# One zero region of a decode backward kernel, written by a memory-to-memory copy on 4 rows and two smaller stores

## The chip, the cores and the metric

The kernel runs on one core of one Trainium2 chip. The metric is device time in microseconds (us) of one execution; lower is better. Times of the kernel before are given as the median of three executions.

## The reference, cut to what matters

One decode step of a block with attention over a sliding window and a gated feed-forward network, and its gradients. Only the last W = 1024 of Sk = 4096 rows of the caches take part:

```python
W = min(4096, max(256, Sk // 4))
k = jnp.repeat(k_cache[:, :, Sk - W:, :], rep, axis=1)
v = jnp.repeat(v_cache[:, :, Sk - W:, :], rep, axis=1)
...
_out, _vjp = jax.vjp(_f, A_x, A_k_cache, A_v_cache, A_wq, A_wo, B_w_gate, B_w_up, B_w_down)
_grads = _vjp(grad_out)
return (_out0, *[jnp.asarray(_g) for _g in _grads])
```

B = 4 sequences, 8 kv-heads, 32 query heads, head size 128, all bf16. Outputs are y, dx, dK cache (`out_2`), dV cache (`out_3`), dWq, dWo and the three feed-forward weight gradients. The gradients of the caches have the full shape (4, 8, 4096, 128). Their first K0 = Sk - W = 3072 rows of each sequence and kv-head are zero, because those rows don't take part. These zeros are 2 x 32 x 3072 x 128 x 2 bytes = 50.3 MB (32 stores of 1536 KB) of the 81.01 MB that the kernel writes.

## The kernel before

**Tiling.** The attention part runs in NT = 4 steps `t` of GP = 2 kv-heads each. A step loads K and V of its two heads (one DMA of 1 MB each per head for all four sequences), transposes the blocks on TensorE (L352), makes scores and the gradient of the probabilities (L345), runs the softmax chain on small tiles, and gives back dK and dV blocks (`dvdk`, L475) and the weight gradients (`dw`, L498). The feed-forward network comes ahead of it, with the same scheme.

**Stores.** Every store goes through `store` (L100). It issues a DMA from SyncE (SP) with `dma_start` and declares that stores of the groups "rest" and "zeros" write disjoint parts of the outputs. dK and dV are gathered in a staging tile `stg`, of which there are three (L719); a tile is stored with one DMA of 1 MB when all JQ blocks are in it (L487 to L489), and its next user waits for that DMA.

**Zeros.** `ztile` (L158) is one SBUF tile of zeros, 128 partitions of 12 KB. `zlist` (L159) lists 32 regions (tensor, sequence, pair of kv-heads). `zero(n)` (L161) takes the next n regions off its left end and writes each with one DMA of 1536 KB, 128 rows of 12 KB, all from `ztile`. The calls of `zero` are spread over the program by hand: ahead of the loads, after each dK and dV store (L490), in the background pieces of the feed-forward network, a group of four in the last step (L734), and what is left at the end (L755).

**Order.** Work that may run in the gaps of other work is put as small functions in the queue `bg`; `tick(n)` (L262) takes n of them. `chain` and `link` do the same for the softmax steps. In the last step, t = 3, the order around the change is: the second K/V pass `kv_steps(t, 1, 1)` (L732) with the pieces of dK and weights of step 2 in its gaps, then `zero(4)` (L734), then the rest of the chain, `softmax_d`, `odq` and `fin` with the dV pieces of step 3 in the gaps. The first dV store of step 3 follows the four zero stores on SP. After the loop, `tick(len(bg))` (L754) gives the last dK and weight pieces.

**Queue.** SP issues its DMAs in program order and waits ahead of each for what it needs. Eight completion semaphores are used in turn for the DMAs issued from SP and ScalarE, and a DMA waits until the earlier DMA on its semaphore has landed. The last two results, `out_b` (L769) and `dx_b` (L787), 4 rows of 1 KB each, are issued from ScalarE.

Of the kernel before, what the change touches and what calls it, by code (L numbers as in the profile page):

```python
# [14 lines left out]
P = 128  # L15
# [3 lines left out]
def kernel(  # L19
# [28 lines left out]
    nc = tc.nc  # L48

    B, Sq, D = A_x.shape  # L50
    _, G, Sk, Dh = A_k_cache.shape
# [4 lines left out]
    K0 = Sk - W  # L56
# [43 lines left out]
    def store(eng, out, in_, kind):  # L100

        eng.nop()
        d = eng.dma_start(out=out, in_=in_)
        for k in ("rest", "zeros") if kind == "rest" else ("rest",):
            tc.declare_no_dep(d.ins, group=k, reason="stores write disjoint parts of the outputs")
        tc.add_to_no_dep_group(kind, d.ins)
        return d
# [12 lines left out]
    def load_w(t, eng=nc.gpsimd):  # L120
        pool = w_pool[t % 2]
        wo_t[t] = pool.tile([P, HG, D], BF16, name="wo_sb", tag="wo")
        eng.dma_start(out=wo_t[t][:], in_=wo_v[t])
        wq_t[t] = pool.tile([P, ND, CW], BF16, name="wq_sb", tag="wq")
        eng.dma_start(out=wq_t[t][:], in_=wq_v[t])

    def load_kv(t, k):
        if t >= NT:
            return
        d_, src, nm = ((k_t, A_k_cache, "kb"), (v_t, A_v_cache, "vb"))[k]  # L130
        for g in range(GP):
            tl = kv_pool[t % 2].tile([P, JB, Dh], BF16, name=nm, tag=nm)
            nc.sync.dma_start(out=tl[:].rearrange("p j d -> p (j d)"),
                              in_=src[:, t * GP + g, K0:Sk, :].rearrange("b (m j) d -> m b (j d)", j=JB))
            d_[(t, g)] = tl
# [22 lines left out]
    ztile = const.tile([P, ZW], BF16, name="ztile")  # L158
    zlist = deque((og, b, g) for b in range(B) for g in range(0, G, ZR) for og in (out_2, out_3))  # L159

    def zero(n=1):  # L161
        for _ in range(min(n, len(zlist))):
            og, b, g = zlist.popleft()
            store(nc.sync, og[b, g:g + ZR, 0:K0, :].rearrange("g (m j) d -> m g (j d)", m=P // ZR), ztile[:], "zeros")


    nc.gpsimd.memset(ztile[:], 0.0)
    zero(3)
    ident_f = const.tile([P, P], FP32, name="ident_f")
    nc.vector.tensor_copy(out=ident_f[:], in_=ident[:])  # L170
# [91 lines left out]
    def tick(n):  # L262
        for _ in range(min(n, len(bg))):
            bg.popleft()()
# [3 lines left out]
    def link(n=1):  # L268
        for _ in range(min(n, len(chain))):
            chain.popleft()()  # L270
# [64 lines left out]
    def kv_steps(t, k, links):  # L335

        zt = (qm_all, dom_all)[k][t % 2]
        blks = (k_t, v_t)[k]
        ps = ps_a.tile([P, WQ], FP32, name="S_ps", tag=("S", "dP")[k])
        st[t][("S", "dP")[k]] = ps[:]  # L340

        def mm(g, q, T_sb):
            c0 = SL - 1 - (g * NQ + q)
            for b in range(B):
                nc.tensor.matmul(ps[b * RB:(b + 1) * RB, :], lhsT=zt[:, b * GP + g, c0:c0 + RB],  # L345
                                 rhs=T_sb[:].rearrange("p (x b) -> p b x", b=B)[:, b, :], start=(g == 0 and q == 0),
                                 stop=(g == GP - 1 and q == NQ - 1), tile_position=(0, b * RB))

        last = None
        for g in range(GP):  # L350
            for q in range(NQ):
                T_ps = transposes([blks[(t, g)][:, q * JQ + j, :] for j in range(JQ)], "T")  # L352
                T_sb = tsb.tile([P, JQ * P], BF16, name="T_sb", tag="T")
                evac(T_sb[:], T_ps[:].rearrange("p j x -> p (j x)"), 1024, half=True)
                tick(1)
                link(links)
                if last:
                    mm(*last)
                last = (g, q, T_sb)
                tick(1)  # L360
                link(links)
        mm(*last)
# [104 lines left out]
    def odT(t, k):  # L467
        rows = st[t][("o", "dq")[k]]
        T_ps = transposes([rows[:, g, :] for g in range(GP)], "odT")
        rT = attw.tile([P, GP, B, rep], BF16, name="od_T", tag=f"od_T{k}")  # L470
        for g in range(GP):
            nc.vector.tensor_copy(out=rT[:, g].rearrange("p b r -> p (b r)"), in_=T_ps[:, g, g * 32:g * 32 + B * rep])
        st[t][("oT", "dqT")[k]] = rT
# [243 lines left out]
    with tc.tile_pool(name="kv_b", bufs=GP, reuse_waits="tile") as kv_b, \  # L717
            tc.tile_pool(name="w_b", bufs=1, reuse_waits="tile") as w_b, \
            tc.tile_pool(name="stage", bufs=3, reuse_waits="tile") as stage:  # L719
        kv_pool[1], w_pool[1] = kv_b, w_b  # L720
        zero()
        pre(0)
        load_w(1)
        load_kv(1, 0)
        for t in range(NT):
            kv_steps(t, 0, 0)
            if t == 0:
                zero()
                load_kv(1, 1)
                zero()  # L730
            softmax(t)
            kv_steps(t, 1, 1)  # L732
            if t == NT - 1:
                zero(4)  # L734
            link(len(chain))
            softmax_d(t)
            link()
            odq(t, 0)
            load_kv(t + 2, 1)
            if t + 1 < NT:  # L740
                pre(t + 1)
            link(len(chain))
            odT(t, 0)
            odq(t, 1)
            load_kv(t + 2, 0)
            tick(2)
            odT(t, 1)
            fin(t)
            if t + 2 < NT:
                load_w(t + 2)  # L750
            (k0, k1), (o0, o1, q0, q1) = dvdk(t, 1), dw(t)
            for p in (k0, o0, k1, o1, q0, q1):
                bg.extend(p)
        tick(len(bg))  # L754
        zero(len(zlist))  # L755

        fin_ps = []
        for o in range(2):
            f_ps = ps_w.tile([B, ND, P], FP32, name="f_ps", tag="w")
            for c in range(ND):  # L760
                nc.tensor.transpose(f_ps[:, c, :], acc[:, o, c, :], ident_f[:])
            fin_ps.append(f_ps)
        acc_o = fin_ps[0][:].rearrange("b c p -> b (c p)")
        acc_d = attw.tile([B, P, ND], FP32, name="acc_d", tag="P_s")
        nc.vector.tensor_copy(out=acc_d[:].rearrange("b p c -> b c p"), in_=fin_ps[1][:])
        acc_d = acc_d[:].rearrange("b p c -> b (p c)")
        out_b = attw.tile([B, D], BF16, name="out_b", tag="pT")
        nc.vector.tensor_tensor(out=out_b[:], in0=acc_o, in1=x4[:], op=ALU.add)
        nc.scalar.dma_start(out=out_0.rearrange("b s d -> (b s) d"), in_=out_b[:])  # L769

        s1 = attw.tile([B, 1], FP32, name="s1", tag="m")
        nc.vector.reduce_sum(out=s1[:], in_=acc_d, axis=AX.X)
        pr = attw.tile([B, D], FP32, name="pr", tag="dS_s")
        s2 = attw.tile([B, 1], FP32, name="s2", tag="es")
        nc.vector.tensor_tensor_reduce(out=pr[:], in0=acc_d, in1=xn_f[:], scale=1.0, scalar=0.0,
                                       op0=ALU.mult, op1=ALU.add, accum_out=s2[:])
        nm1 = attw.tile([B, 1], FP32, name="nm1", tag="rr")
        nc.vector.tensor_scalar(out=nm1[:], in0=s1[:], scalar1=-1.0 / D, scalar2=None, op0=ALU.mult)
        nm2 = attw.tile([B, 1], FP32, name="nm2", tag="gs")
        nc.vector.tensor_scalar(out=nm2[:], in0=s2[:], scalar1=-1.0 / D, scalar2=None, op0=ALU.mult)  # L780
        nc.vector.scalar_tensor_tensor(out=pr[:], in0=xn_f[:], scalar=nm2[:, 0:1], in1=acc_d,
                                       op0=ALU.mult, op1=ALU.add)
        nc.vector.tensor_scalar(out=pr[:], in0=pr[:], scalar1=nm1[:, 0:1], scalar2=rstd[:, 0:1],
                                op0=ALU.add, op1=ALU.mult)
        dx_b = attw.tile([B, D], BF16, name="dx_b", tag="E_f")
        nc.vector.tensor_tensor(out=dx_b[:], in0=pr[:], in1=dy4[:], op=ALU.add)
        nc.scalar.dma_start(out=out_1.rearrange("b s d -> (b s) d"), in_=dx_b[:])  # L787
# [30 lines left out]
```

## Time and profile before

| what | value |
|---|---|
| times of three executions | 282.87, 282.91, 283.6 us; median 282.91 us |
| profiled execution, its own time | 283.0 us |
| span of its instructions | 281.0 us |
| busy: TensorE / VectorE / ScalarE / GpSimd | 203.1 / 164.1 / 117.8 / 40.1 us |
| moved by the DMA engines | 112.12 MB, mean 399 GB/s |
| HBM read / written by the program | 30.68 / 81.01 MB |
| zero stores | 32 of 1536 KB, median 18.1 us from issue to landing |
| granted TensorE clock | 0.901 of full speed |

The span runs from the first to the last instruction that the profile shows; the time of the execution is 2.0 us longer. A DMA's "landing" is the time at which the last of its 16 completion counts arrived. The core has 16 DMA engines. Each DMA is cut into packets, one row of the transfer or part of it per packet, and the trace records start, duration, size and queue of each packet, but not the engine that moved it.

### The profile page before, as it was taken

To read this page: it belongs to the slowest core of one execution; us is meant where nothing else is said; L and a number is where in the kernel's file an instruction comes from. 1 tells how busy PE (TensorE), PEld (TensorE's weight loads), DVE (VectorE), ACT (ScalarE), POOL (GpSimd) and SP (SyncE) were. 2 spreads that over 40 slices of the span, in tenths; PEclk is the share of its full clock that TensorE was granted. 3 is DMA by queue.
4 is the path that set the end of the run, shared out by engine and by line. 5 is a ranking of instruction groups with operands and counts; after the bars stand their busy time and mean duration, and the time that the engine had idled before them with its cause. 6 is when DMAs were issued, how large, how long until landed. Compare 5 with 4: busy or idle time off the path is not lost.

```text
span 281.0 us, 6867 instructions
## 1 busy us (share of the span) xinstructions
PE 203.1 (72%) x2972; PEld 138.8 (49%) x2972; DVE 164.1 (58%) x313; ACT 117.8 (42%) x219; POOL 40.1 (14%) x40
## 2 busy tenths in 40 slices
PE   0276699959789889998999299898999599390000
PEld 0265476735456665566775156677556484140000
DVE  7946646645776655577666067767677728386000
ACT  2030386635035418764448056443866038370000
POOL 8600000007002150002250000223000400000000
PEclk9999589986999999999999969999999979977555
DMA  7999999999999999999999999999999999999990
GB/s 264 393 375 431 431 426 417 425 419 424 369 395 424 422 420 420 426 415 422 419 417 411 412 424 423 431 383 398 385 368 415 387 432 410 425 429 422 398 422 30
DMA packets 19565, 112.12 MB, mean 399 GB/s; under 512 B 1664, under 2 KB 4496, under 8 KB 11088
## 3 DMA queue, kind: packets, MB, share of 16 engines
q1 hardware_dynamic: 17744, 103.56, 89.6%
q0 software_dynamic: 1632, 6.29, 5.6%
q10 hardware_dynamic: 160, 1.84, 1.9%
q8 instruction: 23, 0.38, 0.5%
q14 instruction: 6, 0.05, 0.0%
HBM read 30.68 MB, written 81.01 MB: 397 GB/s over the span
## 4 chain that ended last, share of the span: by engine, by line
PE 47%; DMA 22%; DVE 16%; ACT 4%; issue 2%; SPq 0%; DVEq 0%; ACTq 0%
DMA out_dram<-stg_dv 13%; PE T_ps L279 8%; PE kv_ps L484 7%; DMA wd_sb<-in_B_w_down_dram 6%; PE S_ps L345 5%; PE od_ps L450 5%; DMA out_dram<-osb_g 4%; DVE T_sb L98 3%; DVE dS_s L367 2%; PE wdT_ps L279 2%; PE dwq_ps L520 2%; PE acc_ps L256 2%; PE dwd_ps L660 2%; DVE P_s L367 2%; PE wgT_ps L279 2%
## 5 line engine op out<-in xcount | busy, mean ns | idle before, releaser
L98 DVE COPY T_sb<-T_ps 128x1024 bf16<-128x1024 bf16 x64 | 44.1, 688 | 26.7 <-PE T_ps L279 26.5
L97 ACT CAST stg_dk<-kv_ps 128x512 bf16<-128x512 f32 x52 | 29.2, 588 | 31.2 <-PE kv_ps L484 12.4
L97 ACT CAST stg_dv<-kv_ps 128x512 bf16<-128x512 f32 x51 | 28.1, 588 | 24.9 <-PE kv_ps L484 24.3
L484 PE MATMUL kv_ps<-qmr,dS_s 128*128 128x512 bf16 x64 | 23.9, 414 | 11.3 <-ACT stg_dk L97 10.6
L463 POOL TENSOR_TENSOR o_s<-od_r,msk_r 128x512 bf16<-128x512 bf16 x8 | 9.1, 1157 | 110.2 <-DVE od_r L455 80.9
L484 PE MATMUL kv_ps<-domr,P_s 128*128 128x512 bf16 x64 | 21.3, 382 | 0.0
L279 PE MATMUL T_ps<-ident,vb 128*128 128x128 bf16 x256 | 20.3, 225 | 0.4 <-DVE T_sb L98 0.4
L279 PE MATMUL T_ps<-ident,kb 128*128 128x128 bf16 x256 | 20.4, 225 | 0.0
L279 PEld LDWEIGHTS <-kb 128*128 128x128 bf16 x256 | 17.5, 101 | 4.5 <-issue 1.3
L279 PEld LDWEIGHTS <-vb 128*128 128x128 bf16 x256 | 17.2, 101 | 5.0 <-issue 3.2
L97 ACT CAST osb_q<-dwq_ps 128x512 bf16<-128x512 f32 x25 | 14.6, 587 | 8.3 <-PE dwq_ps L520 7.4
L329 POOL TENSOR_TENSOR domr<-r,msk 128x1024 bf16<-128x1024 bf16 x4 | 7.6, 1892 | 71.2 <-DVE r L326 65.1
L97 ACT CAST osb_g<-dwg_ps 128x512 bf16<-128x512 f32 (+1 forms) x25 | 12.3, 544 | 12.3 <-PE dwg_ps L673 6.3
L97 ACT CAST osb_o<-dwo_ps 128x512 bf16<-128x512 f32 x24 | 13.9, 586 | 4.5 <-PE dwo_ps L505 2.9
L98 DVE CAST stg_dk<-kv_ps 128x512 bf16<-128x512 f32 x12 | 8.0, 688 | 12.0 <-DMA out_dram<-stg_dv 11.2
L98 DVE COPY wgT<-wgT_ps 128x1024 bf16<-128x1024 bf16 x14 | 9.6, 686 | 6.8 <-PE wgT_ps L279 6.8
L345 PE MATMUL S_ps<-T_sb,qm 128*32 128x256 bf16 x128 | 12.7, 387 | 0.6 <-DVE T_sb L98 0.5
L345 PE MATMUL S_ps<-T_sb,dom 128*32 128x256 bf16 x128 | 12.7, 388 | 0.1
L505 PE MATMUL dwo_ps<-dyr,o_s 128*128 128x512 bf16 x32 | 12.4, 413 | 0.3 <-ACT stg_dk L97 0.2
L98 DVE COPY woT<-woT_ps 128x1024 bf16<-128x1024 bf16 x16 | 11.0, 686 | 2.7 <-PE woT_ps L279 2.3
L484 PEld LDWEIGHTS <-dS_s 128*128 128x128 bf16 x64 | 6.2, 101 | 12.2 <-issue 11.1
L520 PE MATMUL dwq_ps<-od_r,xnm 128*128 128x256 bf16 x64 | 11.6, 274 | 0.3 <-ACT osb_q L97 0.2
(188 smaller groups left out, 385.0 us busy)
## 6 DMA issues: line engine op xcount, KB each, us to landing
out_dram<-ztile SPq DMA_DIRECT2D x32, 1536.0 KB, 18.1
kb<-in_A_k_cache_dram SPq DMA_DIRECT2D x8, 1024.0 KB, 17.4
vb<-in_A_v_cache_dram SPq DMA_DIRECT2D x8, 1024.0 KB, 20.7
out_dram<-stg_dv SPq DMA_DIRECT2D x8, 1024.0 KB, 13.0
out_dram<-stg_dk SPq DMA_DIRECT2D x8, 1024.0 KB, 20.8
out_dram<-osb_o SPq DMA_DIRECT2D x8, 512.0 KB, 17.4
out_dram<-osb_q SPq DMA_DIRECT2D x8, 512.0 KB, 13.8
out_dram<-osb_g SPq DMA_DIRECT2D x8, 448.0 KB, 14.3
```

What stands on the lines that cost most here:

```text
L97: return nc.scalar.copy(out=out, in_=in_)
L98: return nc.vector.tensor_copy(out=out, in_=in_)
L256: nc.tensor.matmul(ps[:, c, :], lhsT=lf(c), rhs=rhs, start=(k == 0), stop=(k == len(terms) - 1))
L279: nc.tensor.transpose(ps[:, i, :], a, ident[:])
L329: nc.gpsimd.tensor_tensor(out=mr[:].rearrange("p g q d -> p (g q) d"), in0=r4[:, k, :].unsqueeze(1).broadcast_to([P, SL, Dh]), in1=msk[:]. ...
L345: nc.tensor.matmul(ps[b * RB:(b + 1) * RB, :], lhsT=zt[:, b * GP + g, c0:c0 + RB], rhs=T_sb[:].rearrange("p (x b) -> p b x", b=B)[:, b, :] ...
L367: nc.vector.scalar_tensor_tensor(out=out[:], in0=src[:].unsqueeze(2).broadcast_to([P, WQ, B]), scalar=rr[:, 0:1], in1=mskb[:].unsqueeze(1) ...
L450: nc.tensor.matmul(od_ps[g * 32:g * 32 + B * rep, k, g, :], lhsT=cols[:, jj, g * NQ + q, :], rhs=blks[(t, g)][:, j, :], start=(j == 0), st ...
L463: nc.gpsimd.tensor_tensor(out=o_s[:, g], in0=rows[:, g].unsqueeze(1).broadcast_to([P, rep, Dh]), in1=msk_r[:].unsqueeze(2).broadcast_to([P ...
L484: nc.tensor.matmul(mps[:].rearrange("p q d -> p (q d)"), lhsT=src[:, j * P:(j + 1) * P], rhs=mr[:, g].rearrange("p q d -> p (q d)"), start ...
L505: nc.tensor.matmul(mps[:], lhsT=o_s[:, g].rearrange("p r d -> p (r d)")[:, i:rep * Dh:rep], rhs=dyr[:], start=True, stop=True)
L520: nc.tensor.matmul(mps[:, i].rearrange("p g d -> p (g d)"), lhsT=xnm[:, i2 * 2 + i, c * P:(c + 1) * P], rhs=dq_r[:].rearrange("p g d -> p ...
```

## The change

The group of four zero stores in the last step becomes three, and the last region of the list, `out_3[3, 6:8]`, is taken off the right end of the list and written in three parts by a new function.

```diff
+    def zero_4():
+
+        og, b, g = zlist.pop()
+        assert og is out_3
+        k0 = 3 * K0 // 4
+        d_, s_ = (x[0:k0, :].rearrange("(c m j) d -> m c (j d)", m=4, c=3) for x in (og[b, g], out_2[0, 0]))
+        store(nc.sync, d_, s_, "zeros")
+        if k0 < K0:
+            w = (K0 - k0) // P
+            store(nc.sync, og[b, g, k0:K0, :].rearrange("(m j) d -> m (j d)", m=P), ztile[:, 0:w * Dh], "zeros")
+        w = K0 // P
+        store(nc.sync, og[b, g + 1, 0:K0, :].rearrange("(m j) d -> m (j d)", m=P), ztile[:, 0:w * Dh], "zeros")
...
             if t == NT - 1:
-                zero(4)
+                zero(3)
+                zero_4()
             link(len(chain))
```

The first part is a copy from memory to memory: rows 0 to 2303 of kv-head 6 are copied from the same rows of `out_2[0, 0]`, which the first zero store of the program wrote. The transfer has 4 rows of 3 pieces, each piece 192 x 128 bf16 = 48 KB, 576 KB in all. The second part, the other 768 rows of kv-head 6, goes from `ztile` as 128 rows of 1.5 KB, 192 KB in all. The third part, kv-head 7, goes from `ztile` as 128 rows of 6 KB, 768 KB in all. The number of zero bytes written stays 1536 KB; 576 KB more are read from HBM. Because the copied region comes from the right end of the list, the region that `zero(4)` took fourth is written by the next `zero` call, and so on to the end; each later call of `zero` writes another region of the same size. The last `zero(len(zlist))` still has two regions.

## Prediction

> **What bounds the kernel now.** I read the DMA rows of the page first, because nearly all of the work that surrounds the change is stores.
>
> ```profile
> span 281.0 us, 6867 instructions
> DMA  7999999999999999999999999999999999999990
> GB/s 264 393 375 431 431 426 417 425 419 424 369 395 424 422 420 420 426 415 422 419 417 411 412 424 423 431 383 398 385 368 415 387 432 410 425 429 422 398 422 30
> q1 hardware_dynamic: 17744, 103.56, 89.6%
> ```
>
> The 16 DMA engines are busy from the second slice to the last but one, at 370 to 430 GB/s, while TensorE, the busiest compute engine, has 72%. So the end is set by bytes per DMA engine. Next I cut the tail into stretches (the windows view):
>
> ```profile
> 251.00:260.00 9.00, 1.86 (x14) 1.07 (x13) 6.50 (x13) 1.01 (x2) 0.00 (x0) 0.77 1.03 429
> 260.00:269.00 9.00, 0.00 (x0) 0.00 (x0) 0.00 (x0) 0.00 (x0) 0.00 (x0) 0.50 1.01 409
> 269.00:274.00 5.00, 0.00 (x0) 0.00 (x0) 0.00 (x0) 0.00 (x0) 0.00 (x0) 0.50 0.99 417
> 274.00:276.00 2.00, 0.00 (x0) 0.00 (x0) 0.00 (x0) 0.00 (x0) 0.00 (x0) 0.50 0.15 61
> 276.00:279.00 3.00, 0.00 (x0) 0.00 (x0) 0.00 (x0) 0.00 (x0) 0.00 (x0) 0.50 0.06 25
> ```
>
> The last two columns are the DMA share and GB/s. All compute is over by 260. Until 274 all engines move data; from 276 to 279 the share is 0.06, which is 1/16: **one engine** still works, at 25 GB/s. The DMA view of the same stretch (275.9 to 279.6) confirms it:
>
> ```profile
> DMA packets 10, 0.10 MB, mean 27 GB/s; under 512 B 2, under 2 KB 2, under 8 KB 2
> q1 hardware_dynamic: 10, 0.10, 6.2%
> ```
>
> Ten packets, 0.10 MB: the eight rows of 12 KB that one engine has of the last zero store, and two counts. This engine is not late by accident of the last store. From the trace's records of completion counts I sorted the 16 arrivals of each DMA (us; "12 x" is a group within 0.3 us):
>
> ```
> issued  DMA            arrivals
> 222.77  zeros    12 x 236.7..237.0, 238.0, 238.7, ... last 242.9
> 233.63  stg_dv   12 x 239.2..239.5, 240.5, 241.1, 241.3, last 245.3
> 242.94  zeros    12 x 255.4..255.5, 256.4, 256.9, 257.0, last 261.5
> 263.85  zeros    12 x 274.4..274.7, 274.9, 275.4, 275.5, last 279.9
> ```
>
> The last engine is 4.0 to 4.5 us behind the next one in each of them, 5 to 6 us behind the group of 12, from about 150 us on. I call it the straggler. It never idles, so its bytes set the end: 279.9, and 1.1 us later the span is over at 281.0. The SP waits show what else hangs on it:
>
> ```profile
> SPq L103 <- DMA out_dram<-ztile: 5.5, 2, 3.2
> SPq L103 <- DMA out_dram<-stg_dv: 3.8, 2, 2.0
> ```
>
> and the chain of waits has, at 233.63, the DMA that ended last before the final dK pieces:
>
> ```profile
> 233.63 11.70 DMA out_dram<-stg_dv
> 245.42 0.59 ACT stg_dk L97
> ```
>
> A landing is the straggler's arrival (245.3), so staging buffers and semaphores come free when the straggler is done. The queue still holds 10 us and more of work at that time, so these waits cost nothing now.
>
> **What the Trainium skill says.** "DMA: Bandwidth & Descriptors", section "Why a DMA increments its semaphore by 16 and not by 1": a DMA is split over the largest k up to 16 that divides the slowest dimension, and a DMA from SP or ScalarE takes the lowest-numbered k engines. The copy's slowest dimension is 4, so it goes to 4 engines. The trace agrees so far: `out_b` and `dx_b`, 4 rows each, left 8 packets of 1024 B at the end, no more. The section "Queues, rings and completion order" says that each DMA engine works its queue in order; the arrivals above keep the order of issue on every place of the sort. The section "Latency and other measured facts" has copies between HBM tensors at 214 GB/s per direction at full rate with 16 KB rows. No run here shows a copy from memory to memory.
>
> **Are the 4 engines free of the straggler?** Packets of `out_b` start at 258.821, 258.833, 258.838 and 258.881 on the 4 engines. The straggler's packets there are isolated (12 KB rows of the store issued at 242.94, when all others are past it): 258.753 to 259.213, next start 259.209, no room for a packet between. For `dx_b` (262.125 to 262.320) it moves 4 KB rows back to back, 261.991, 262.146, unstretched at 159 ns. So it carried neither. The four starts also lie where the group of 12 changes to its next DMA (258.874 to 258.982). So the copy's engines very likely belong to the group of 12, which ends 5.5 us early.
>
> **The change part by part** (profiled execution, arrivals as above).
> 1. *One 1536 KB store less.* Each engine loses 8 packets of 12 KB. Packets follow one another at (279.571 - 275.915)/8 = 0.457 us: 3.66 us less on each.
> 2. *The two stores from the tile.* Each engine gets 8 packets of 1.5 KB and 8 of 6 KB. Spacings in the trace (duration less 3.5 ns overlap) are 0.4565 us for 12 KB, 0.3055 for 8 KB, 0.1555 for 4 KB, 0.0805 for 2 KB, so about 0.0055 + 0.0367 per KB: 0.231 and 0.061 us by this line. 8 x 0.292 = 2.33 us more. Net on each engine, straggler included: **-1.32 us**.
> 3. *The copy.* 576 KB on 4 engines are 144 KB each. At the rate of the 12 KB rows, 12 x 0.457 = 5.48 us; in longer pieces by the line above 144 x 0.0367 = 5.29. I take 5.4. At half the rate, from the skill's 214 GB/s over 16 engines = 13.4 GB/s each, an estimate, 147,456 B take 11.0 us. Below 5.3 us I see no way, as no packet size in this trace passes 27 GB/s per engine. I choose 5.4, because every kind of transfer here, load or store, runs at the same 26.8 GB/s per engine (8 KB in 309 ns both ways), which looks like a limit of the engine and not of an end; with 4 engines only, the traffic of memory grows little. Both ends stay in the range.
> 4. *SP.* Six DMAs in place of four, two more issues of about 0.5 to 1.4 us each as in the SP timeline. They lie between 224.1 (end of the fourth issue) and 233.6, where SP waits for the dV piece anyway (7.5 us, "DVE stg_dv"): nothing. Without that cover it would be 1 to 3 us of the issue order, still behind a queue of over 10 us. The source of the copy was written by the first zero store, which landed near 40 us, so no wait from that; back-to-back zero stores at 219.7 to 224.1 show that disjoint regions of one output don't wait for each other.
> 5. *What is queued behind the copy.* All later stores reach these 4 engines later by 5.4 - 1.3 = 4.1 us. The first dV store then arrives there at about 239.3 + 4.1 = 243.4, and on the straggler at 245.3 - 1.3 = 244.0. The straggler still ends the landing, 1.3 us earlier, so the waits for `stg`, for semaphores, and the release of the final pieces move forward with it. Two more DMAs move the turn of the eight semaphores by two places: a later DMA may wait on one of the small stores instead of a zero store, and these land no later.
>
> **Sum.** The four engines end at 274.4 - 1.3 + 5.4 = 278.5, the straggler at 279.9 - 1.3 = 278.6; span 278.6 + 1.1 = 279.7, 1.3 less. Against the profiled 283.0 that is 281.7, and against the median of 282.91, which lies 0.1 lower, **281.6**. The end after the change is nearly level between straggler and copy engines: more gain isn't there in this split, and every loss of copy speed shows at once.
>
> **The rivals.**
> - *The copy runs at half rate.* For it: the skill's figure, and that both sides of the transfer are memory. Against: the equal rates of loads and stores. The 4 engines end at 274.4 - 1.3 + 11.0 = 284.1, 4.2 past the old end: 287.1, slower. They are the new stragglers, the dV store lands at 239.3 + 9.7 = 249.0, and the final dK pieces start 3.6 us later. The turning point is a copy of 5.4 + 1.4 = 6.8 us, 22 GB/s per engine.
> - *In between,* 18 to 24 GB/s or memory contention slowing all 16 engines: a copy of 6.1 to 8.2 us, 282.2 to 284.3; middle near 283.
> - *The change doesn't steer:* the copy spreads over 12 or 16 engines, all get nearly the old bytes, and the straggler keeps its lead: about 282.9.
> - *The straggler is one of the four:* its load grows by 4.1 us: 287.0. The `out_b` packets speak against it.
>
> **How the numbers follow.** Forecast 0.54, half rate 0.27, in between 0.11, no steering 0.04, straggler hit 0.04. About 0.3% (0.85 us) is what a measurement can tell from no change, so faster by that needs a copy under 5.8 us: nearly all of the forecast's chance and none of the rest, 0.51. Same: 0.03 of the forecast, 0.06 of the in-between case, the unsteered 0.04, together 0.13. Slower: 0.27 + 0.05 + 0.04 = 0.36. The forecast's own range is 281.0 to 282.4 (copy 5.3 to 6.1 us, and 0.6 us below for a straggler lag that differs between executions). Both signs being likely, the whole range reaches the half-rate case: 281.0 to 287.2.
>
> **What would show it.** Right: the share of 1/16 at the end gives way to about five engines that finish together within 0.5 us near 278.6; the copy's packets take 5.4 us per engine; the first dV store of step 3 lands 1.3 us earlier. Wrong: packets of the copy at 13 GB/s, four arrivals after all others in every later DMA, and "ACT stg_dk <- DMA stg_dv" at about 8 us in place of 4.6. Also wrong if the straggler's lag isn't there in another execution; then the copy only adds 4.1 us to four engines and the end is later.

## The result and the profile after

The changed kernel takes 282.37 us (median of 20 runs) against 283.36 us (20 runs) for the kernel before: ratio 0.9962, 95% interval 0.9951 to 0.9973, so 1.08 us less (0.77 to 1.39). The forecast was 1.3 us less, a ratio of 0.9954, inside the interval. The median of before was 282.91 in the first three runs and is 283.36 over twenty, which is why 281.6 was 0.8 us too low as an absolute time while the difference was missed by 0.2 (by 0.3 if the medians are subtracted).

The profiled execution of the changed kernel took 283.39 us (span 281.4 us). It was already about 1 us behind the profiled execution of before when the change begins (the last store ahead of it is issued at 220.43 in place of 219.31), so ends are compared inside each trace, with the group of engines that ends first, and times by the ratios.

The windows view of the tail, columns as before with DMA share and GB/s last:

```profile
269.00:274.00 5.00, 0.00 (x0) 0.00 (x0) 0.00 (x0) 0.00 (x0) 0.00 (x0) 0.50 0.99 411
274.00:276.00 2.00, 0.00 (x0) 0.00 (x0) 0.00 (x0) 0.00 (x0) 0.00 (x0) 0.50 0.35 147
276.00:279.00 3.00, 0.00 (x0) 0.00 (x0) 0.00 (x0) 0.00 (x0) 0.00 (x0) 0.50 0.30 127
```

From 276 to 279 the share is 0.30 in place of 0.06: 0.30 x 16 = 4.8, five engines in place of one. This is the straggler and the four copy engines, as the prediction asked for. The issues of the stretch 219 to 283 show the three new DMAs with their sizes:

```profile
out_dram<-ztile SPq DMA_DIRECT2D x1, 768.0 KB, 17.0
out_dram<-out_dram SPq DMA_DIRECT2D x1, 576.0 KB
out_dram<-ztile SPq DMA_DIRECT2D x1, 192.0 KB
```

The chain of waits has the first dV store of the last step again, 11.42 us from issue to landing in place of 11.70:

```profile
234.63 11.42 DMA out_dram<-stg_dv
246.16 0.59 ACT stg_dk L97
```

The arrivals of completion counts, sorted as in the prediction (us):

```
issued  DMA                   arrivals
220.43  osb_q (before copy)   14 x 223.0..223.3, 224.6, last 228.0
226.52  zeros, 6 KB rows      9 x 236.6..237.0, 237.8, 238.5, 242.3, 4 x 243.3..243.5
264.30  zeros (the last)      8 x 274.0..274.2, 274.6, 274.9, 275.2, 279.3, 4 x 280.3..280.5
```

Ahead of the copy there is one late engine. After it there are one and four. The four end the kernel, 1.1 us after the straggler and not level with it. The packet records show where the time goes. The copy's pieces are packets of 49,152 B. Eight of the twelve take 1815 to 1834 ns, which is 27 GB/s, the rate of the other stores. The other four, one on each engine, take 2284 to 2462 ns. And the last two 12 KB rows ahead of the copy take 880 to 907 ns in place of 460 on each of the four engines. Behind the copy the four are 6.8 us behind the leading group (243.4 less 236.6), of which the bytes of the copy are 3 x 1.813 = 5.44: about 1.4 us beyond the bytes.

### The profile page after: what moved, and what is told of

Same layout as the page of the kernel before. It is cut to its first block, busy times and chain, and to the rows that moved or that the text cites. A ratio compares the mean times of both kernels' runs of the same rounds, so it can differ in the third digit from the quotient of the medians.

```text
span 281.4 us, 6867 instructions
## 1 busy us (share of the span) xinstructions
PE 203.2 (72%) x2972; PEld 138.5 (49%) x2972; DVE 164.1 (58%) x313; ACT 117.4 (42%) x219; POOL 40.1 (14%) x40
## 4 chain that ended last, share of the span: by engine, by line
DMA 39%; PE 36%; DVE 11%; ACT 3%; issue 2%; SPq 0%; DVEq 0%; ACTq 0%
DMA out_dram<-stg_dv 21%; DMA out_dram<-osb_o 9%; PE T_ps L292 6%; DMA wd_sb<-in_B_w_down_dram 6%; PE kv_ps L497 5%; PE S_ps L358 4%; DMA out_dram<-osb_g 4%; PE od_ps L463 4%; PE dwd_ps L673 2%; PE wgT_ps L292 2%; DVE T_sb L98 2%; PE dwq_ps L533 2%; PE wdT_ps L292 2%; PE dwg_ps L686 2%; PE acc_ps L269 1%
```

## The experiments

All are edits of the changed kernel's `zero_4`, each timed against the kernel before. In all of them "straggler" is the one engine that is late ahead of the copy.

**First group: does the gain come from who carries the bytes, and what does the copy cost?**

*Half of the head on the four rows.*

```diff
-        k0 = 3 * K0 // 4
+        k0 = K0 // 2
```

> Half of the kv-head is copied on the 4 rows (three pieces of 32 KB each, 96 KB per engine) in place of three quarters; the other half goes from the tile as rows of 3 KB. Steering theory (the end is the later of the straggler and the four copy engines): the straggler loses 24 KB = 0.9 us in place of 1.3; the copy engines get 3.6 us of copy plus about 1.4 us of the slowing seen in the changed kernel's profile, and end at 274.4 - 0.9 + 5.0 = 278.5, about level with the straggler at 279.9 - 0.9 = 279.0. Gain about 0.9 us over the kernel before, as large as that of the changed kernel (ratio 0.996 to 0.998). If the copy ran without extra cost and the straggler alone set the end of the changed kernel, this one would be 0.4 us slower than it. Rival (the gain comes from bytes that leave the tile's side for memory, not from who carries them): gain two thirds of the changed kernel's, 0.7 us.

Measured: 282.24 us, ratio 0.9961 (0.9948 to 0.9974), as large a gain as that of the change. In its profile the four end at 278.4 to 278.6 and the straggler at 279.0, level as expected. Behind the copy the four are 5.2 us behind the leading group, of which 96 KB are 3.6: again about 1.6 us beyond the bytes. Steering explains it; the rival's 0.7 us (0.9975) lies just outside the interval, so the next run has to decide.

*The same bytes copied on 16 rows.*

```diff
-        d_, s_ = (x[0:k0, :].rearrange("(c m j) d -> m c (j d)", m=4, c=3) for x in (og[b, g], out_2[0, 0]))
+        d_, s_ = (x[0:k0, :].rearrange("(c m j) d -> m c (j d)", m=16, c=1) for x in (og[b, g], out_2[0, 0]))
```

> The same 576 KB copied from memory, but on 16 rows of 36 KB, so every engine carries its share of 36 KB. Steering theory: the straggler keeps its bytes, so the gain is gone: the time of before, within 0.3 us, or up to 0.5 us slower if copied bytes cost more than bytes from the tile. Rival (copying from memory is itself cheaper, or the smaller stores are): the gain of about 1 us stays, ratio near 0.996.

Measured: 283.53 us, ratio 0.9999 (0.9984 to 1.0014). The gain is gone. In the tail (windows view)

```profile
271.00:275.00 4.00, 0.00 (x0) 0.00 (x0) 0.00 (x0) 0.00 (x0) 0.00 (x0) 0.50 0.98 417
277.20:280.80 3.60, 0.00 (x0) 0.00 (x0) 0.00 (x0) 0.00 (x0) 0.00 (x0) 0.50 0.06 24
```

one engine works alone again, share 0.06, until 281.0, 5.7 us after the leading group. Copying from memory, larger pieces and the split into three DMAs bring nothing by themselves: it is the straggler's bytes. This excludes the rival.

*Without the copy.* The 576 KB are not written at all.

```diff
-        d_, s_ = (x[0:k0, :].rearrange("(c m j) d -> m c (j d)", m=4, c=3) for x in (og[b, g], out_2[0, 0]))
-        store(nc.sync, d_, s_, "zeros")
```

> The copy is left out and nothing writes its 576 KB (rows 0 to 2303 of one kv-head of the dV cache); the rest is as in the changed kernel. Steering theory: every engine loses 36 KB, the straggler sets the end alone, 1.3 us before the old end: ratio 0.995; this is the most that the changed kernel could reach, and the difference to it is what the copy costs at the end. If the copy engines end the changed kernel about 1 us behind the straggler, as in its profile, this kernel is 0.5 to 1 us faster than it. Rival (the copy is hidden entirely): the two are equal within 0.3 us.

Measured: 282.06 us, ratio 0.9948 (0.9932 to 0.9964), 1.5 us less than before (1.0 to 1.9). The tail is that of one engine (windows view):

```profile
269.00:272.00 3.00, 0.00 (x0) 0.00 (x0) 0.00 (x0) 0.00 (x0) 0.00 (x0) 0.50 1.01 427
274.00:276.00 2.00, 0.00 (x0) 0.00 (x0) 0.00 (x0) 0.00 (x0) 0.00 (x0) 0.50 0.06 25
276.00:278.00 2.00, 0.00 (x0) 0.00 (x0) 0.00 (x0) 0.00 (x0) 0.00 (x0) 0.50 0.07 31
```

So the 1.3 us of the straggler are right, and the changed kernel gives back 0.4 us (282.37 less 282.06 is 0.3; the ratios say 0.14%), less than the 0.5 to 1 us that were expected. The two intervals overlap, so the size of what is given back is an indication; that the copy engines end behind the straggler is seen in the trace.

*15 engines from the tile.* These lines stand in `zero_4` in place of all that follows its `zlist.pop()`.

```diff
+        k0 = 15 * K0 // 16
+        store(nc.sync, og[b, g:g + ZR, 0:k0, :].rearrange("g (m j) d -> m g (j d)", m=60), ztile[0:120, :], "zeros")
+        w = (K0 - k0) // 64
+        store(nc.sync, og[b, g:g + ZR, k0:K0, :].rearrange("g (m j) d -> m g (j d)", m=64), ztile[:, 0:w * Dh], "zeros")
```

> No copy: the region is written from the tile as 120 rows of 12 KB, which divides over 15 engines and not over 16, and a rest of 128 rows of 0.75 KB. If the straggler is the highest-numbered engine, it loses 96 KB and gains 6 KB: 3.4 us less, while the others gain 0.3 us: end at 279.9 - 3.4 = 276.5, gain 3.4 us, ratio 0.988, and in the profile the last engine ends about 1 us behind the group. If the straggler is another of the engines 4 to 14, nothing moves off it: 0.3 us slower than before, and one engine ends 5 us before the group instead.

Measured: 287.76 us, ratio 1.0154 (1.0132 to 1.0175), 4.4 us slower, which neither case foresaw. One engine did skip the store (first arrival of the next DMA at 233.8, the next at 237.6), and it was not the straggler, which still came last. But all the engines that took part lost time: of the 12 KB rows that started between 230 and 246 us, 89 took more than 600 ns, up to 1769, against 9 in the changed kernel and 1 in the kernel before. The straggler needed 7.0 us from one landing to the next (240.1 to 247.1) for a store whose rows should take 3.7. A store from SBUF on 120 partitions is not a 128-row store with one engine left out. It isn't the uneven split alone: the kernels with copies from memory on 5, 6 and 7 rows below have 9 to 12 such rows. The cause stays open; nothing here measured it.

**Second group: which engine is it, and what beats the change?**

*A whole head copied on 8, on 12 and on 4 rows,* and the changed kernel a second time. The edit for 8 rows is shown; the others have m=12, c=2 and m=4, c=4.

```diff
-        k0 = 3 * K0 // 4
-        d_, s_ = (x[0:k0, :].rearrange("(c m j) d -> m c (j d)", m=4, c=3) for x in (og[b, g], out_2[0, 0]))
+        k0 = K0
+        d_, s_ = (x[0:k0, :].rearrange("(c m j) d -> m c (j d)", m=8, c=2) for x in (og[b, g], out_2[0, 0]))
```

> A whole kv-head (768 KB) is copied, on 8 rows of two 48 KB pieces, so eight engines carry 96 KB each and all engines lose 48 KB against the kernel before. Steering theory with the cost of the copy as measured so far (its bytes at the rate of the tile's rows plus about 1.4 us per engine): if the straggler is none of the eight lowest engines, it ends 1.8 us earlier and the copy engines at 274.4 - 1.8 + 3.6 + 1.4 - 0.5 = 277.1, so gain 1.8 us, ratio 0.9937, faster than the changed kernel. If the straggler is one of engines 4 to 7, it ends 1.8 to 3.2 us later: ratio 1.006 to 1.011.

> The same kv-head (768 KB) copied on 12 rows of two 32 KB pieces, 64 KB on each of twelve engines. If the straggler is above the twelve lowest engines, it ends 1.8 us earlier as in the run with 8 rows and nothing else is near the end: ratio 0.9937. If it is one of the twelve, it ends 0.6 to 2.0 us later than before: ratio 1.002 to 1.007. With the run on 8 rows this places the straggler among engines 4 to 7, 8 to 11 or 12 to 15.

> The same kv-head (768 KB) copied on 4 rows of four 48 KB pieces, 192 KB on each of four engines. Theory that the copy engines set the end from three quarters on: they end at 274.4 - 1.8 + 7.3 + 1.4 - 0.5 = 280.8, 0.9 us after the old end: ratio about 1.003, and 1.3 to 1.9 us slower than with three quarters. If the copy had no cost beyond its bytes and started at once (the rate of the prediction), they would end at 279.9, level with the kernel before: ratio 1.000.

> The changed kernel once more, for a second profile and in the company of the other splits. Theory: the four copy engines end last, 0.5 to 1 us after the straggler, as in its first profile, and the ratio is again 0.996. If in this execution the straggler ends last, which of the two sets the end differs from execution to execution.

Measured: 8 rows 285.01 us, ratio 1.0063 (1.004 to 1.0086); 12 rows 283.86, 1.002 (1.0007 to 1.0032); 4 rows 284.21, 1.0021 (1.0008 to 1.0035); the changed kernel again 282.33, 0.9963 (0.995 to 0.9976). On 8 and 12 rows the straggler carries a row, and the trace shows it directly: of the eight rows of 8, seven begin at 234.2 to 234.5 and one at 239.77. On 4 rows none begins late. So the straggler is one of engines 4 to 7, if engines are counted from 0 and a transfer on k rows takes the k lowest, as the prediction assumes; the trace itself does not name the engine. The whole head on 4 rows overloads the four: they end at 281.3 to 281.4, the straggler at 279.4, and the gain turns into a loss. The second profile of the changed kernel has the same order as the first: straggler 278.6, copy engines 279.5 to 279.6.

*On 7, 6 and 5 rows.* The edit for 5 rows is shown. For 6 rows it is k0 = K0 with m=6, c=4, for 7 rows k0 = 14 * 216 with m=7, c=2, and the 48 rows left of the head from the tile on 16 rows.

```diff
-        k0 = 3 * K0 // 4
-        d_, s_ = (x[0:k0, :].rearrange("(c m j) d -> m c (j d)", m=4, c=3) for x in (og[b, g], out_2[0, 0]))
+        k0 = 5 * K0 // 6
+        d_, s_ = (x[0:k0, :].rearrange("(c m j) d -> m c (j d)", m=5, c=4) for x in (og[b, g], out_2[0, 0]))
```

> 3024 rows of the kv-head (756 KB) copied on 7 rows of two 54 KB pieces, 108 KB on each of the seven lowest engines; the last 48 rows go from the tile on 16 rows. The straggler carried a row when the copy had 8 or 12 rows and none when it had 4, so it is one of engines 4 to 7. If it is engine 7: it ends 1.8 us earlier and the copy engines at 274.4 - 1.8 + 4.0 + 1.4 - 0.5 = 277.5, gain 1.8 us, ratio 0.9937, faster than the changed kernel. If it is engine 4, 5 or 6: 2.2 us later than before, ratio 1.008.

> The whole kv-head (768 KB) copied on 6 rows of four 32 KB pieces, 128 KB on each of six engines. If the straggler is engine 6 or 7: straggler and copy engines both end near 278.2, gain 1.6 us, ratio 0.994. If it is engine 4 or 5: 3.0 us later than before, ratio 1.010.

> Five sixths of the kv-head (2560 rows, 640 KB) copied on 5 rows of four 32 KB pieces, 128 KB on each of the five lowest engines. The straggler carried a row with 6 and 7 rows, and none with 4, so it is engine 4 or 5. If it is engine 5: it loses 40 KB = 1.5 us, the copy engines end at 274.4 - 1.5 + 4.8 + 1.4 - 0.5 = 278.6, both near 278.5; gain 1.3 to 1.4 us, ratio 0.9953, a little faster than the changed kernel. If it is engine 4: it ends 3.3 us later than before, ratio 1.0115, and four rows are the most that can be copied past it.

Measured: 7 rows 285.53 us, ratio 1.0088 (1.0071 to 1.0106); 6 rows 286.28, 1.0103 (1.009 to 1.0116); 5 rows 286.34, 1.0112 (1.0089 to 1.0134). All are slower, so the straggler carries a row as soon as there are five: by the same counting it is the fifth engine, number 4. With 5 rows the tail shows the order:

```profile
275.60:278.00 2.40, 0.00 (x0) 0.00 (x0) 0.00 (x0) 0.00 (x0) 0.00 (x0) 0.50 0.32 138
279.00:283.00 4.00, 0.00 (x0) 0.00 (x0) 0.00 (x0) 0.00 (x0) 0.00 (x0) 0.50 0.06 25
```

five engines work at first (0.32), then one alone (0.06): the other four copy engines are done at 278.8 and the straggler, with its own row of the copy, at 283.3. Four rows are the most that can be copied past it, and no version here beats the change; the copy of half a head does as well.

**The cost beyond the bytes.** *Pieces of 12 KB.*

```diff
-        d_, s_ = (x[0:k0, :].rearrange("(c m j) d -> m c (j d)", m=4, c=3) for x in (og[b, g], out_2[0, 0]))
+        d_, s_ = (x[0:k0, :].rearrange("(c m j) d -> m c (j d)", m=4, c=12) for x in (og[b, g], out_2[0, 0]))
```

> The changed kernel's 576 KB on 4 rows, but each row in twelve pieces of 12 KB, as large as the rows of the other zero stores. In the changed kernel the copy costs an engine 1.4 us beyond its bytes: two rows of the store ahead take 907 ns in place of 460, and one 48 KB piece takes 0.5 to 0.65 us longer. Theory that the size of the pieces makes this cost (a long piece stands in the way of the packets beside it): it shrinks below 0.5 us, the copy engines end before the straggler, and the gain grows to 1.3 us, ratio 0.9954 or below. Rival (it comes with any copy from memory to memory on an engine, whatever its pieces): two rows ahead at about 907 ns again, copy engines again 0.5 to 1 us behind the straggler, ratio 0.996.

Measured: 282.42 us, ratio 0.9968 (0.9956 to 0.998). Seven of the rows ahead of the copy take 907 ns again and an eighth 873, the four copy engines are 6.8 to 6.9 us behind the leading group after the copy, as with 48 KB pieces, and they end at 279.8 to 279.9 beside the leading group's 273.5. The size of the pieces doesn't make the extra 1.4 us. The rival's last point did not come true: the straggler ended at 279.75, level with the copy engines. It was already 6.1 us late ahead of the change in this execution, against 4.9 in the first profile of the changed kernel.

## Why the prediction was right, and which term was mis-sized

1. **The bound.** Right. One engine's bytes set the end. The table takes the net bytes that each kernel gives the straggler, at 0.0375 us per KB, against two measurements: the time that the straggler itself needs in the trace, from its arrival of the last `osb_q` store ahead of the change to its end (52.6 us in the kernel before), and the measured difference of the kernel. The first is free of what happened ahead of the change.

| kernel | net on the straggler | by the line | straggler's time in the trace | measured (ratio x 283.3) |
|---|---|---|---|---|
| without the copy | -36 KB | -1.3 us | -1.3 us | -1.5 us |
| copy on 16 rows | 0 | 0.0 | +0.1 | 0.0 |
| 12 rows | +16 KB | +0.6 | +0.6 | +0.6 |
| 8 rows | +48 KB | +1.8 | +1.8 | +1.8 |
| 7 rows | +61 KB | +2.3 | +2.4 | +2.5 |
| 6 rows | +80 KB | +3.0 | +3.0 | +2.9 |
| 5 rows | +88 KB | +3.3 | +3.4 | +3.2 |

With 4 rows the copy engines end last or within 0.6 us of the straggler, so the kernel's time tells less; the straggler's own time follows all the same: -0.9 us with half a head, -1.3 in both profiles of the changed kernel (-1.5 with small pieces) and -1.8 with the whole head, for -24, -36 and -48 KB.

2. **The straggler is none of the four.** Right, as read from where the packets of `out_b` and `dx_b` fell. It is the very next engine, so there was no room to spare. The Trainium skill's page "DMA: Bandwidth & Descriptors", section "Why a DMA increments its semaphore by 16 and not by 1", says that k is the largest divisor of the slowest dimension up to 16 and that the engines are the lowest-numbered. That fits all seven row counts: a late row appears from 5 rows on and not with 4.

3. **Straggler -1.32 us.** Right: 1.3 us in the traces, and 1.5 us (1.0 to 1.9) by the time of the kernel without the copy. The rows of 1.5 and 6 KB took 65 and 234 ns, close to the estimate.

4. **The copy at 5.4 us.** Its rate was right: 1815 ns per 48 KB piece, 27.1 GB/s per engine, 5.44 us for three. The rival of half rate didn't happen. Its 13.4 GB/s per engine was an estimate from the 214 GB/s that the Trainium skill's page "DMA: Bandwidth & Descriptors" gives in the section "Latency and other measured facts"; for four engines this estimate doesn't hold. With 16 engines copying (the 16-row kernel) eight of the 36 KB pieces take 1364 to 1433 ns and eight take 1779 to 2785 ns, so more of the copy is slow when more engines copy at once. The lower bound of 5.29 us came from a slip: the four spacings that the prediction lists give 0.0375 us per KB and not 0.0367, which makes 5.40; its sum of 2.33 us for the small stores was made with the right slope.

   Mis-sized was the term: behind the copy an engine has lost about 6.8 us, not 5.4, because about 1.4 us come on top, once per copy and whatever its bytes: 1.6 for 96 KB, 1.4 and 1.5 for 144 KB (1.4 in 12 KB pieces), 1.4 for 192 KB. Two rows of the store ahead at twice their time are 0.9 of it, one stretched piece the other 0.5. What it is, I can't say. It falls on engines that copy at the same time: in the six kernels in which the straggler has a row of the copy, some 5 us after the others, its time in the trace is within 0.1 us of its bytes. In the 8-row kernel it copied its two pieces in 3.73 us, 0.1 above the bytes, while five of the others took 4.30 to 4.40 (pieces alone, without the slowed rows ahead).

5. **"The four engines end level with the straggler."** This is the step that failed in size. They end 0.9 to 1.1 us after it in both profiles. Counted like the straggler's time above, the leading group of the kernel before needs 52.5 us and the copy engines 57.3 and 57.4, so 4.8 to 4.9 us more and not 4.1.

   By the prediction's own sum a copy of 6.8 us is the turning point, at which no gain is left. Two things kept one. At the end the copy engines are 6.3 us behind the leading group and no longer 6.8; the straggler of the kernel before gains on that group as well, from 6.1 to 5.5 us, so this is not a property of the copy. And the straggler's lag differs: ahead of the change, where all the kernels here are the same program, it was 4.9 to 6.1 us in the 14 profiled executions. The gain is then this lag and 52.6 us, less the 57.3 us of the copy engines, and at most the 1.3 us of the straggler: 0.2 to 1.3 us, about 0.8 on average, an estimate from single traces; measured 1.08 (0.77 to 1.39). So what bounds the end was understood, but that the forecast of 1.3 us came so close was in part luck.

   Its three signs of being right came only in part: the five engines are there, but end 1.1 us apart and not within 0.5, and the copy's pieces take 5.9 to 6.2 us per engine in the two profiles and not 5.4. The third, a dV landing 1.3 us earlier, did not come (point 6). One sign of being wrong did come: the copy engines are the last four arrivals of every later DMA, 0.8 to 1.4 us after the straggler. The wait for dV did not grow to 8 us, as the waits views of 219 to 283 show (us in total, times, longest):

```profile
ACT stg_dk L97 <- DMA out_dram<-stg_dv: 4.3, 1, 4.3
SPq L103 <- DMA out_dram<-out_dram: 1.0, 1, 1.0
```

6. **SP, semaphores and landings.** Six issues fit into the wait for dV, as said, and no wait on the copy's source appears (the copy is issued at 223.88, right behind the third zero store). The second line above is a wait that the prediction did not have: SP waited 1.0 us for the copy's own landing before it issued a dK store, because the two share a semaphore. The chain after the dV store moved by 0.3 us, 11.70 to 11.42, not by 1.3, because the copy engines now land last. Neither shows an effect on the end.

7. **Small slips.** The first of the sorted arrivals has 13 and not 12 engines in its group. The straggler's distance to the next engine is not steady from 150 us on: it is 4.2 us at 151, 1.9 at 165 to 170, and 4 to 4.5 again in the stretch that counts. And a gain of 0.85 us needs, by the prediction's sum, a copy under about 5.9 us, not 5.8.

## What to carry to other kernels

When a DMA-bound kernel ends with a share of 1/16, look at the sorted arrivals of each DMA: one late engine sets the end, and a transfer whose slowest dimension is small takes bytes off it and gives them to engines that end early, as long as the late one isn't among those that carry it. Count the engines' ends afterwards, both the late one's and the new carriers'; by the sum the best split is where they meet, and half and three quarters of a head, on either side of it here, did equally well. Read which engine is late before choosing the number of rows, since one row too many turned 1 us of gain into 3 us of loss.

## What the runs showed that was not expected

- A copy from memory to memory costs each of the engines that copy at the same time about 1.4 us beyond its bytes, of which 0.9 us fall on the two rows of the store ahead of it (880 to 907 ns in place of 460). Pieces of 12, 32 and 48 KB make no difference to this. The straggler, which copies about 5 us after the others, pays no more than 0.1 us. What the cost is stays open.
- A store of the same 12 KB rows on 120 partitions of the tile in place of 128 made the kernel 4.4 us slower, with 89 rows above 600 ns in place of 9. The cause stays open.
- The late engine is number 4 in every kernel here that tells, counted as above. Why it is late stays open; in the trace of before its distance to the next engine grows from 1.3 us to 4.2 us between 140 and 151 us, far ahead of the change, and no run looked for its cause.
